# Top-32 attention with a squared-ReLU feed-forward: order of the last step and the tail, place of the negation, of a cast and of the threshold tests, and the step from which a DMA does an addition

## The chip, the cores and the metric

The kernel runs on one core of a Trainium2 chip. Its five engines work from queues of their own: TensorE (PE; its weight loads are shown as PEld), VectorE (DVE), ScalarE (ACT), GpSimd (POOL) and SyncE (SP, which here only issues DMAs). The metric is the device time of one execution in microseconds, as the median over runs.

## The reference

For each of 8 batches and 8 heads, 576 queries meet 576 keys of 64 dimensions. Of each row of scores only those stay that are at least as large as the row's 32nd largest; a softmax over them weighs the values. The result, 4608 tokens of 512 features, goes through a feed-forward with the square of a ReLU:

```python
scores = scale * np.matmul(q, k.transpose(0, 1, 3, 2))
kth = np.partition(scores, -top_k, axis=-1)[..., -top_k:-top_k + 1]
scores = np.where(scores >= kth, scores, -1000000000.0)
attn = np.exp(scores - np.max(scores, axis=-1, keepdims=True))
attn = attn / (np.sum(attn, axis=-1, keepdims=True) + 1e-09)
x = np.matmul(attn, v)            # then heads side by side: 4608 x 512
h = np.maximum(x @ w_in, 0.0)     # 4608 x 2048
out = h * h @ w_out               # 4608 x 512
```

## The kernel before

The work is cut into 144 steps (`U`). A step handles two tiles (`x` = 0, 1) of 128 queries against 576 keys. One loop over `u` writes each engine's order by hand (`pin` keeps the program order), and several steps are in flight at once.

- **Selection, DVE.** `pairs_of` and `quads_of` (L314 to L324) fold the scores by maxima and minima, so that the first of four rounds need to read only part of a row. `topk` then does four rounds of MAX8 (L373) with MATCH_REPLACE8 between (L377); the last value of the fourth round is the row's threshold. `lesser` and `both` (POOL, L347 and L338) make the smaller elements of the pairs, which the fourth round reads as well. `copy_far` (ACT, L330) saves a part (`most`) that would be overwritten in PSUM.
- **Mask, POOL.** In step u, `drop(u-1, x)` turns the threshold into a mask: `negate` (ACT, L392) gives the negatives of the row's largest value and of its threshold (`neg`); L407 on POOL writes a byte that is large where a score lies below the threshold; and that byte, read as a bfloat16 of huge magnitude, is added to the scores `s`. In steps below `EARLY` = 11 (and in the second-last step) POOL adds it itself, one L409 for each tile. Otherwise one DMA with accumulation, issued by POOL, does it for both tiles (L411).
- **Softmax and values.** `exps(u-2)` (ACT, L415) exponentiates, `turn` transposes by DMA on SP's queue (L424), `products(u-4)` (PE, L459) multiplies by the values, `invert` and `place` (DVE L473, ACT L489) normalise. In the last two steps tiles that POOL doesn't mask go through `early_exps` (ACT, L400) and `mask` (DVE, L419), and are transposed on PE (`turn_by_tensor`, L441; `turned` copies them out, L446 and L448).
- **Preparation of the next heads.** `prep_units` transposes queries and keys on PE (L174) and copies them on ACT (L175). `main` also hands a cast of the last values, `last_values` (ACT, L221), to the list `after_far`, which the same step empties after its fourth round.
- **Feed-forward.** When a block of 128 tokens is complete, `x_unit` transposes it (L527) and `block` makes four "ups" (16 matmuls each, L574, then `rl` by ACT L579 and the square) and four "downs" (4 matmuls each, L617, into the one bank `dn_ps`; after the fourth it is copied to `wide`, L625 or L623, and stored). `piece` takes one from the lists `ups` and `downs`, in turn; `dense(u, 0)` and `dense(u, 1)` call it at the end of every step. `piece(True)` leaves the evacuation for later, in the list `behind`. Blocks of 64 remaining rows of two batches go through `rem_unit`.
- **Tests.** Every 18 steps (`GROUP`) three POOL instructions (L382 to L384) compare the thresholds of the rounds and write to `flags`. At the very end DVE reduces `flags` (L855); a positive value would start a general path, which doesn't run on this data.
- **Tail.** After the loop come the masks of the last tiles, their transposes, products and placing, the last ups and downs, and the last block's downs in two halves of 256 columns (`halves`, L598).

Of the kernel before, what the change touches and what calls it, by code (L numbers as in the profile page):

```python
# [23 lines left out]
def kernel(  # L24
# [9 lines left out]
    nc = tc.nc  # L34
# [10 lines left out]
    def pin(ins):  # L45
        tc.keep_in_program_order(ins)
        return ins
# [43 lines left out]
    raw, prep = {}, {}  # L91

    fetches = []
    after_far = []

    def by_head(t):
        return t.rearrange("p (a d) -> p a d", a=2)
# [61 lines left out]
    def prep_units(i):  # L159
# [10 lines left out]
        def main(which, src):  # L170
            def go():
                tp = ps_one.tile([128, 512], f32, name="gen", bufs=2)
                for c in range(4):
                    pin(nc.tensor.transpose(tp[:, c * 128:(c + 1) * 128], src[:, c], id_f[:, :]))  # L174
                pin(nc.scalar.activation((qT, kT[:, 64:576])[which], tp[:, :], AF.Copy, scale=(scale, 1.0)[which]))  # L175
                after_far.append(lambda: last_values(which))
            return go


# [38 lines left out]
        def last_values(x):  # L218
            assert i < 6 or av_left[i - 6] == 0
            half = slice(64 * x, 64 * x + 64)  # L220
            pin(nc.scalar.activation(va[half, 4 + x, :, 0:64], by_head(v_raw[half, 512:640]), AF.Copy))  # L221
# [127 lines left out]
    GROUP = 18  # L349
    EARLY = 11  # L350
    held_m = {}

    def topk(u, rounds=(0, 1, 2, 3)):
        d = st[u]
        g = u % GROUP
        if g == 0 and 0 in rounds:
            held_m["m"] = small.tile([128, GROUP, 2, 4, 8], f32, name="m", bufs=2)
        held = held_m["m"]  # L360
        m = d["m"] = [held[:, g, :, r] for r in range(4)]
        d["ends"] = held[:, g].rearrange("p x r j -> p x (r j)")[:, :, 0:32:31]
        cat = d["cat"]
        def part(r, x):
            if r == 0:
                return cat[:, x, 0:QUAR].rearrange("p (g n) -> p g n", n=18)[:, :, 0:13]
            if r == 1:
                return cat[:, x, 0:QUAR].rearrange("p (g n) -> p g n", n=6)[:, :, 1:6]
            return cat[:, x, 0:(HALF - 24, S)[r - 2]]

        for r in rounds:
            for x in range(2):
                pin(nc.vector.max(out=m[r][:, x, :], in_=part(r, x)))  # L373
            if r == 3:
                break
            for x in range(2):
                pin(nc.vector.match_replace(out=part(r, x), in_to_replace=m[r][:, x, :], in_values=part(r, x), imm_value=NEG))  # L377
        if g == GROUP - 1 and 3 in rounds:
            f0 = 2 * (u + 1 - GROUP)
            each = held[:, :, :, :, 7].rearrange("p g x r -> p (g x) r")  # L380
            at = flags[:, f0:f0 + 2 * GROUP]
            pin(nc.gpsimd.tensor_tensor(at[:, :, 0:3], each[:, :, 3:4].broadcast_to([128, 2 * GROUP, 3]), each[:, :, 0:3], op=ALU.subtract))  # L382
            pin(nc.gpsimd.tensor_mul(at[:, :, 3], each[:, :, 3], each[:, :, 3]))
            pin(nc.gpsimd.tensor_scalar(at[:, :, 3], at[:, :, 3], scalar1=-1.0, scalar2=TINY * TINY, op0=ALU.mult, op1=ALU.add))  # L384

    def by_vector(u, x):
        return u == U - 1 or (u == U - 2 and x == 1)
# [13 lines left out]

    def drop(u, x):
        d = st[u]
        if x == 0:
            d["neg"] = negate(u, 2)
        s, byte = d["s"], gone[u % 2]
        pin(nc.gpsimd.tensor_scalar(byte[:, x, :, 1], s[:, x, :], scalar1=d["neg"][:, x, 1:2], scalar2=-HUGE, op0=ALU.add, op1=ALU.mult))  # L407
        if by_vector(u, 1) or u < EARLY:
            pin(nc.gpsimd.tensor_tensor(s[:, x, :], s[:, x, :], byte[:, x, :, :].rearrange("p n two -> p (n two)").bitcast(bf16), op=ALU.add))  # L409
        elif x == 1:  # L410
            pin(nc.gpsimd.dma_start(out=s[:, :, :].rearrange("p x n -> p (x n)"), in_=byte[:, :, :, :].rearrange("p x n two -> p (x n two)").bitcast(bf16), accum_op=ALU.add))  # L411
# [328 lines left out]
    def ok(w):  # L740
        return 0 <= w < U
# [16 lines left out]
    for u in range(U):  # L758
        at_step[0] = u
        for x in range(2):  # L760
            if ok(u - 1) and not by_vector(u - 1, x):
                drop(u - 1, x)
        quads_of(u)
        topk(u, (0,))
        if u == U - 1:
            products(u - 4)
        if ok(u + 1):
            for i, c, a in steps[u + 1]:
                while coming <= i or (coming == i + 1 and soon):
                    prepare(u)  # L770
            scores(u + 1, (lambda: in_gap(u)) if u else None)
            both(u + 1)
        if u == 0:
            in_gap(u)
        if ok(u - 4):
            invert(u - 4)
        casts_next = bool(soon) and soon[0].__name__ == "values"
        for _ in range(0 if casts_next else 2 if u < 8 else 1):
            prepare(u)
        if ok(u - 4):  # L780
            place(u - 4)
        turn_x(u)
        moves.extend(soon_moves)
        soon_moves.clear()
        if u == U - 1:
            moves.pop(0)()()
        if ok(u - 2):
            exps(u - 2, 0)
            exps(u - 2, 1)
            turn(u - 2)  # L790
        fetch(4 if u < 12 else 3)
        topk(u, (1, 2))
        if ok(u + 1):
            pairs_of(u + 1)
            copy_far(u + 1)
            lesser(u + 1)
        topk(u, (3,))
        if casts_next:
            prepare(u)
        while after_far:  # L800
            after_far.pop(0)()
        if u == U - 2:
            early_exps(u, 1)
        if u < U - 1:
            dense(u, 0)
            dense(u, 1)
        else:
            early_exps(u, 0)
            exps(u - 1, 0)
            early_exps(u, 1)  # L810
            piece(True)
            piece(True)
        load_weights(1)
    mask(U - 2, 1)
    mask(U - 1, 0)
    mask(U - 1, 1)
    while_scores.close()
    ends["pool"] = fast.enter_context(tc.tile_pool(name="ps_end", bufs=1, space=PSUM))

    def flush():  # L820
        if behind:
            behind.pop(0)()

    assert not fresh and not moves and not soon_moves
    late.append(True)
    products(U - 4)
    piece(True)
    behind.sort(key=lambda go: go.down)
    invert(U - 4)
    for u in (U - 2, U - 1):  # L830
        for x in range(2):
            turn_by_tensor(u, x)
            turned(u, x, u == U - 2)
    products(U - 2)
    products(U - 1)
    place(U - 4)
    products(U - 3)
    invert(U - 2)
    flush()
    place(U - 2)  # L840
    invert(U - 1)
    invert(U - 3)
    flush()
    place(U - 1)
    place(U - 3)
    rest = ups.pop(0)()
    turn_x(U)
    moves.pop(0)()()
    rest()
    while behind:  # L850
        flush()
    tail.append(0)
    while ups:
        ups.pop(0)()()
# [141 lines left out]
```

## Time and profile before

| | |
|---|---|
| median of 3 runs | 917.33 us (914.49 to 920.94) |
| profiled execution | 915.97 us, its span 914.1 us |
| granted TensorE clock, mean | 0.942 of full speed |
| DVE busy | 882.7 us (97%) |
| POOL busy | 777.6 us (85%) |
| ACT busy | 760.2 us (83%) |
| PE busy | 675.0 us (74%) |
| DMA moved | 163.60 MB, mean 179 GB/s |

A row of the timeline gives the start, the duration from the first to the last of the merged instructions, the engine, the line, the operation, its output and inputs with shapes, and the count; in brackets the idle time of the engine ahead of it and what ended it. A row of the waits gives who waited for whom: the total in us, how often, and the longest. A row of the windows gives a stretch, its length, the busy time of PE, PEld, DVE, ACT and POOL with counts, the granted PE clock, the busy share of the DMA engines and their GB/s. Lines (L392) are those of the kernel before; in the changed kernel they lie up to five further down.

### The profile page before, as it was taken

What the parts mean: (1) busy time and instruction counts of PE and PEld (TensorE: products, weight loads), DVE (VectorE), ACT (ScalarE), POOL (GpSimd) and SP (SyncE); (2) the same over time, 40 slices, a digit from 0 to 9 for tenths busy, and PEclk for the clock granted to TensorE, in tenths of its full rate; (3) what the DMA queues carried; (4) which work ended last, traced back from release to release, by engine and by line L of the source; (5) the groups of instructions that cost most, each with busy time, mean ns of one, the idle gap of its engine ahead of it and who ended that gap; (6) DMA issues with size and microseconds to landing.
All of it is one profiled execution on the core that took longest, in us unless ns stands there. A gap on an engine that the chain in (4) does not pass through costs nothing.

```text
span 914.1 us, 20885 instructions
## 1 busy us (share of the span) xinstructions
PE 675.0 (74%) x6188; PEld 427.2 (47%) x6264; DVE 882.7 (97%) x3632; ACT 760.2 (83%) x1755; POOL 777.6 (85%) x804
## 2 busy tenths in 40 slices
PE   6667667776786777777786777777777778878776
PEld 3333344544454445444454444454444445545454
DVE  5999999999999999999999999999999999999993
ACT  4566699889888998888987899988998888998881
POOL 7998989888988889888888888998898888888860
PEclk9999999899989999999989999999999999999999
DMA  7698799899998999899899998989989999788851
GB/s 145 106 165 142 155 184 202 192 198 194 193 202 185 196 198 195 190 175 215 178 198 182 202 199 186 205 193 196 185 192 197 199 202 196 156 166 172 163 117 39
DMA packets 290489, 163.60 MB, mean 179 GB/s; under 512 B 258112, under 2 KB 268608, under 8 KB 290368
## 3 DMA queue, kind: packets, MB, share of 16 engines
q1 hardware_dynamic: 267408, 80.29, 47.1%
q0 software_dynamic: 21616, 81.47, 40.0%
q8 instruction: 52, 0.85, 0.4%
q14 instruction: 69, 0.57, 0.2%
q10 hardware_dynamic: 1344, 0.43, 0.2%
HBM read 37.75 MB, written 9.44 MB: 52 GB/s over the span
## 4 chain that ended last, share of the span: by engine, by line
DVE 66%; issue 11%; PE 4%; DMA 3%; ACT 2%; POOL 2%; POOLq 0%; ACTq 0%
DVE m L373 27%; DVE cat L377 18%; DVE sc_b L314 6%; DVE cat L324 5%; DVE cat L323 5%; DVE most L315 4%; DMA s<-gone_a 1%; DMA s<-gone_b 1%; PE dn_ps L617 1%; DVE rsum L473 1%; PE gen L574 1%; PE sc_b L285 1%; POOL gone_b L407 0%; POOL cat L347 0%; PE end L598 0%
## 5 line engine op out<-in xcount | busy, mean ns | idle before, releaser
L373 DVE MAX8 m<-cat 128x8 f32<-128x104 f32 (+3 forms) x1152 | 438.7, 422 | 0.2 <-POOL cat L347 0.2
L377 DVE MATCH_REPLACE8 cat<-m,cat 128x104 f32<-128x104 f32 (+2 forms) x864 | 263.1, 312 | 0.0
L338 POOL TENSOR_TENSOR cat<-s 128x576 int32<-128x576 int32 (+1 forms) x144 | 238.6, 1657 | 3.1 <-ACT s L294 3.1
L347 POOL TENSOR_TENSOR cat<-cat,most 128x576 int32<-128x576 int32 (+1 forms) x144 | 195.8, 1360 | 19.6 <-ACT most L330 7.0
L285 PE MATMUL sc_b<-qkT 64*128 64x288 f32 x512 | 109.1, 501 | 95.3 <-DVE cat L324 91.2
L285 PE MATMUL sc_a<-qkT 64*128 64x288 f32 x512 | 98.2, 456 | 96.6 <-DVE most L315 62.9
L574 PEld LDWEIGHTS <-w_in 128*128 128x128 bf16 x2304 | 146.2, 101 | 39.0 <-issue 17.1
L617 PE MATMUL dn_ps<-w_out,h 128*128 128x512 bf16 x494 | 147.2, 420 | 10.3 <-issue 5.7
L294 ACT ACTIVATE s<-sc_b 128x576 f32<-128x576 f32 x144 | 93.4, 649 | 63.9 <-PE sc_b L285 57.0
L574 PE MATMUL gen<-xT,w_in 128*128 128x128 bf16 x2000 | 138.5, 226 | 2.6 <-ACT xT L533 1.4
L407 POOL TENSOR_SCALAR gone_a<-s,neg 128x576 uint8<-128x576 f32 x143 | 106.6, 745 | 21.3 <-ACT neg L392 10.8
L407 POOL TENSOR_SCALAR gone_b<-s,neg 128x576 uint8<-128x576 f32 x142 | 105.9, 746 | 18.3 <-ACT neg L392 7.7
L285 PEld LDWEIGHTS sc_a<-qkT 64*128 64x128 f32 x512 | 41.8, 188 | 124.2 <-issue 30.7
L285 PEld LDWEIGHTS sc_b<-qkT 64*128 64x128 f32 x512 | 44.7, 201 | 110.7 <-PE av_ps L459 64.1
L294 ACT ACTIVATE s<-sc_a 128x576 f32<-128x576 f32 x144 | 91.0, 632 | 3.3 <-DVE cat L317 1.7
L585 ACT ACTIVATE h<-rl 128x512 bf16<-128x512 f32 x136 | 85.7, 630 | 4.3
L579 ACT ACTIVATE rl<-gen 128x512 f32<-128x512 f32 x141 | 84.0, 596 | 2.4 <-PE gen L574 1.9
L617 PEld LDWEIGHTS <-h 128*128 128x128 bf16 x560 | 54.3, 106 | 66.2 <-issue 32.5
L459 PEld LDWEIGHTS <-wT 128*128 128x128 bf16 (+1 forms) x1600 | 54.9, 100 | 53.6 <-issue 43.9
L411 POOL DMA_DIRECT2D s<-gone_b x66 | 58.4, 884 | 21.7 <-DVE m L373 7.6
L415 ACT ACTIVATE w_two_a<-s,neg 128x576 bf16<-128x576 f32 x96 | 69.4, 781 | 6.7 <-DMA s<-gone_b 4.5
L415 ACT ACTIVATE w_two_c<-s,neg 128x576 bf16<-128x576 f32 x94 | 68.0, 781 | 8.1 <-DMA s<-gone_b 4.7
(170 smaller groups left out, 1203.1 us busy)
## 6 DMA issues: line engine op xcount, KB each, us to landing
s<-gone_b POOLq DMA_DIRECT2D x66, 576.0 KB, 4.6
s<-gone_a POOLq DMA_DIRECT2D x65, 576.0 KB, 4.7
v_raw<-in_v_dram SPq DMA_DIRECT2D x64, 128.0 KB, 3.1
k_raw<-in_k_dram SPq DMA_DIRECT2D x63, 128.0 KB, 3.3
q_raw<-in_q_dram SPq DMA_DIRECT2D x63, 128.0 KB, 3.2
out_dram<-wide SPq DMA_DIRECT2D x31, 256.0 KB, 3.1
v_raw<-in_v_dram SPq DMA_DIRECT2D x64, 32.0 KB, 3.1
w_in<-in_moe_w_in_dram POOLq DMA_DIRECT2D x8, 256.0 KB, 4.8
```

Source lines behind the costliest of these rows:

```text
L285: pin(nc.tensor.matmul(out=ps[j][:, x, 0:HALF], lhsT=lhsT, rhs=rhs, start=True, stop=True))
L294: pin(nc.scalar.activation(s[:, :, j * HALF:(j + 1) * HALF], ps[j][:, :, 0:HALF], AF.Copy))
L338: pin(tt(less, s[:, :, 0:wide].bitcast(i32), s[:, :, HALF:HALF + wide].bitcast(i32), op=ALU.add))
L347: pin(tt(less, less, d["most"][:, 0:n_h, :, :].bitcast(i32).rearrange("p h x n -> p x h n"), op=ALU.subtract))
L373: pin(nc.vector.max(out=m[r][:, x, :], in_=part(r, x)))
L377: pin(nc.vector.match_replace(out=part(r, x), in_to_replace=m[r][:, x, :], in_values=part(r, x), imm_value=NEG))
L407: pin(nc.gpsimd.tensor_scalar(byte[:, x, :, 1], s[:, x, :], scalar1=d["neg"][:, x, 1:2], scalar2=-HUGE, op0=ALU.add, op1=ALU.mult))
L415: pin(nc.scalar.activation(w_two[u % 3][:, x, 0:S], d["s"][:, x, :], AF.Exp, bias=d["neg"][:, x, 0:1]))
L574: pin(nc.tensor.matmul(out=hp[:, n * n_rows:(n + 1) * n_rows], lhsT=w_in[:, kh, (f0 + n) * 128:(f0 + n + 1) * 128], rhs=xt(kh), start=(kh ...
L579: pin(nc.scalar.activation(rl[:, :], hp, AF.Relu))
L585: pin(nc.scalar.activation(h2, flat, AF.Square))
L617: pin(nc.tensor.matmul(out=op[:, :], lhsT=held["h2"][:, f, c * 128:(c + 1) * 128], rhs=w_out[:, f, :], start=(f == 0), stop=(f == NF - 1)))
```

## The change

- The casts of `last_values` go through a second list, `next_far`, and run one step later.
- The three test instructions become five of 128 x 36 elements (`tests`); one runs per step on POOL, after `lesser`; what is left runs after the loop.
- `negate` moves from the start of the next step's `drop` to between `dense(u, 0)` and `dense(u, 1)`.
- The DMA adds the mask from step 9 on (`EARLY - 2`) instead of 11; nothing else that depends on `EARLY` changes.
- In the last step two `piece()` calls stand behind `products(u - 4)`. In the changed order of instructions these are the last two downs of the block of remainder rows, whose copy to `wide` falls to ACT; the two `piece(True)` calls later in the step are then both ups of the second-last block.
- In the tail the `piece(True)` behind `products(U - 4)` is gone, inversions follow their products, one postponed evacuation runs ahead of `place(U - 4)` and one after the transposes of the last block.

```diff
@@ prep_units: main
-                after_far.append(lambda: last_values(which))
+                next_far.append(lambda: last_values(which))
@@ topk
-            pin(nc.gpsimd.tensor_tensor(at[:, :, 0:3], each[:, :, 3:4].broadcast_to([128, 2 * GROUP, 3]), each[:, :, 0:3], op=ALU.subtract))
-            pin(nc.gpsimd.tensor_mul(at[:, :, 3], each[:, :, 3], each[:, :, 3]))
-            pin(nc.gpsimd.tensor_scalar(at[:, :, 3], at[:, :, 3], scalar1=-1.0, scalar2=TINY * TINY, op0=ALU.mult, op1=ALU.add))
+            for r in range(3):
+                tests.append(lambda r=r: nc.gpsimd.tensor_tensor(at[:, :, r], each[:, :, 3], each[:, :, r], op=ALU.subtract))
+            tests.append(lambda: nc.gpsimd.tensor_mul(at[:, :, 3], each[:, :, 3], each[:, :, 3]))
+            tests.append(lambda: nc.gpsimd.tensor_scalar(at[:, :, 3], at[:, :, 3], scalar1=-1.0, scalar2=TINY * TINY, op0=ALU.mult, op1=ALU.add))
@@ drop
-        if x == 0:
+        if "neg" not in d:
             d["neg"] = negate(u, 2)
...
-        if by_vector(u, 1) or u < EARLY:
+        if by_vector(u, 1) or u < EARLY - 2:
@@ the loop over u
         if u == U - 1:
             products(u - 4)
+            piece()
+            piece()
...
             lesser(u + 1)
+            if tests:
+                pin(tests.pop(0)())
         topk(u, (3,))
         if casts_next:
             prepare(u)
         while after_far:
             after_far.pop(0)()
+        after_far.extend(next_far)
+        next_far.clear()
...
             dense(u, 0)
+            st[u]["neg"] = negate(u, 2)
             dense(u, 1)
@@ after the loop
+    while tests:
+        pin(tests.pop(0)())
     mask(U - 2, 1)
...
     products(U - 4)
-    piece(True)
-    behind.sort(key=lambda go: go.down)
-    invert(U - 4)
     for u in (U - 2, U - 1):
         for x in range(2):
             turn_by_tensor(u, x)
             turned(u, x, u == U - 2)
+    invert(U - 4)
     products(U - 2)
+    invert(U - 2)
     products(U - 1)
+    invert(U - 1)
+    behind.pop(0)()
     place(U - 4)
     products(U - 3)
-    invert(U - 2)
-    flush()
     place(U - 2)
-    invert(U - 1)
     invert(U - 3)
-    flush()
     place(U - 1)
     place(U - 3)
-    rest = ups.pop(0)()
+    behind.append(ups.pop(0)())
     turn_x(U)
     moves.pop(0)()()
-    rest()
+    behind.pop(0)()
+    behind.append(ups.pop(0)())
     while behind:
-        flush()
+        behind.pop(0)()
```

More of the change, by code (lines that the diff above doesn't have):

```diff
@@ L93 @@
     fetches = []
-    after_far = []
+    after_far, next_far = [], []
     def by_head(t):
@@ L351 @@
     held_m = {}
+    tests = []
     def topk(u, rounds=(0, 1, 2, 3)):
@@ L818 @@
     ends["pool"] = fast.enter_context(tc.tile_pool(name="ps_end", bufs=1, space=PSUM))
[L820 to L824, printed above, removed]
+    assert not fresh and not moves and not soon_moves and len(behind) == 2 and len(ups) == 2
     late.append(True)
     products(U - 4)
-    piece(True)
-    behind.sort(key=lambda go: go.down)
-    invert(U - 4)
     for u in (U - 2, U - 1):
```

## The prediction

> **What bounds the kernel now.** I read the page first, then stages by windows, the waits of VectorE (DVE), and the instructions in order of time where DVE has gaps.
>
> ```profile
> PE 675.0 (74%) x6188; PEld 427.2 (47%) x6264; DVE 882.7 (97%) x3632; ACT 760.2 (83%) x1755; POOL 777.6 (85%) x804
> ...
> core 0: us, PE busy (x) PEld busy (x) DVE busy (x) ACT busy (x) POOL busy (x), PEclk, DMA share, GB/s
> 0.00:40.00 40.00, 26.24 (x121) 13.43 (x124) 30.81 (x126) 18.64 (x42) 33.31 (x73) 1.00 0.71 130
> 40.00:80.00 40.00, 27.77 (x189) 13.26 (x191) 39.48 (x160) 24.35 (x61) 36.41 (x41) 0.96 0.97 162
> 80.00:120.00 40.00, 27.90 (x242) 16.30 (x244) 37.53 (x153) 29.57 (x71) 36.55 (x35) 0.96 0.73 146
> ...
> 300.00:400.00 100.00, 73.66 (x697) 47.63 (x702) 100.00 (x421) 88.29 (x204) 88.21 (x88) 0.94 0.93 191
> ...
> 880.00:914.00 34.00, 22.98 (x249) 16.66 (x250) 17.50 (x45) 13.07 (x31) 5.44 (x6) 0.89 0.24 51
> ```
>
> DVE is the wall: from 120 to 880 us it hardly pauses (100.00 of 100.00 us in the stretch shown), and the change takes no instruction from it there. So only DVE's 31.4 us of idle time (914.1 - 882.7) can be won: 9.2 us before 40, 0.5 + 2.5 us from 40 to 120, 16.5 us after 880, and what is left of the sum, 2.7 us, in the 760 us between. The head before 40 us waits for first loads and transposes, which the change leaves alone. I cost the rest in three parts: tail, steps 8 to 12, steady steps.
>
> **Tail.** Rows of PE, DVE and ACT in order of time, each engine by itself:
>
> ```profile
> 876.06 1.89 PE L617 MATMUL dn_ps<-w_out,h 128*128 128x512 bf16 x7
> 877.78 0.47 PE L459 MATMUL av_ps<-vau_b,wT 128*128 128x65 bf16 x10
> 881.61 0.43 PE L527 MATMUL gen<-id_h,x_tok 128*128 128x128 bf16 x2 [3.24 <-ACT x_tok L489]
> 887.24 0.67 PE L441 MATMUL end<-id_h,w_two_b 128*128 128x128 bf16 x9
> 891.37 0.55 PE L527 MATMUL end<-id_h,x_tok 128*128 128x128 bf16 x4 [0.51 <-ACT x_tok L489]
> 895.32 1.06 PE L574 MATMUL end<-xT,w_in 128*128 128x128 bf16 x16
> 896.43 0.81 PE L617 MATMUL dn_ps<-w_out,h 128*128 128x512 bf16 x3
> 899.86 5.17 PE L617 MATMUL dn_ps<-w_out,h 128*128 128x512 bf16 x16 [2.62 <-DVE wide L623]
> 904.96 0.19 PE L863 MATMUL gen<-ones,worst 128*1 128x1 f32 x2
> ...
> 885.50 1.76 DVE L419 SCALAR_TENSOR_TENSOR w_two_c<-s,m,e 128x576 bf16<-128x576 f32 x2
> 897.66 1.34 DVE L855 TENSOR_REDUCE worst<-flags 128x1 f32<-128x1152 f32 x1
> 899.11 0.69 DVE L623 COPY wide<-dn_ps 128x512 f32<-128x512 f32 x1
> ...
> 881.24 0.52 ACT L489 ACTIVATE x_tok<-av_ps,rsum 128x64 bf16<-128x64 f32 x2 [0.68 <-DVE rsum L473]
> 889.13 0.62 ACT L579 ACTIVATE rl<-gen 128x512 f32<-128x512 f32 x1
> 889.61 0.55 ACT L489 ACTIVATE x_tok<-end,rsum 128x64 bf16<-128x64 f32 x2
> ...
> 896.30:899.80 3.50, 0.89 (x5) 0.31 (x4) 3.26 (x5) 0.60 (x1) 0.00 (x0) 0.98 0.02 5
> 899.80:905.00 5.20, 5.14 (x18) 1.86 (x17) 0.01 (x1) 0.00 (x0) 0.00 (x0) 0.69 0.23 50
> ```
>
> Today the third-last block of the feed-forward (the remainder rows) leaves its last four L617 matmuls (896.43; the profile lost one) for after the last L574 group. The next block's sixteen need the same single dn_ps bank, and its copy L623 stands on DVE behind the reduction L855, so PE waits 2.62 us. In the changed order of instructions all eight remaining L617 matmuls stand in the last step ahead of the x_tok transposes, their copy on ACT. Three gains follow.
>
> *Queue.* The sixteen then follow the L574 groups: they start where the four start now, 899.86 - 896.43 = 3.43 us earlier. What was moved is covered: eight L617 take 877.78 - 876.06 = 1.72 us at full clock, and PE is idle 3.24 us ahead of 881.61; the copy (0.69 us on DVE, about as much on ACT) falls into ACT's 0.68 us wait ahead of 881.24. Without that cover the x_tok chain would lose at most that 0.7.
>
> *Clock.* The sixteen took 904.96 - 899.86 = 5.10 us at a granted clock of 0.69; at the rate of the eight they take 2 x 1.72 = 3.44. With no wait in front of them I expect the full rate: 1.66 us. If the clock is low for another reason: 0.
>
> The Trainium skill ("TensorE: Matmul & The Clock Gate", "What's actually happening") says that the clock falls after an idle window of about 3.4 us, free-running. A wait of 2.62 us doesn't fill one, so read strictly the slow sixteen would have another cause and stay slow, and the whole sum below would be 7.3 instead of 9.0. The trace, 0.98 in the stretch up to the end of the wait and 0.69 behind it, speaks for the wait.
>
> *Front.* Two L574 groups of the second-last block run in the last step, one after the other, instead of one, four L617 and another; the transposes L441 of w_two_b, today at 887.24, can start up to 0.9 us earlier. Those of the last half of w_two_c still wait for the last mask (885.50 + 1.76 = 887.26). Only one of the two postponed rl evacuations stands ahead of the last x_tok on ACT instead of two (889.61 - 889.13 = 0.48 us). I bound the gain at 891.37 by 0 (mask alone) and 0.48 + 0.62 = 1.1 (a whole evacuation as well) and take 0.8, nearer the upper end since both chains shorten.
>
> Tail: 3.43 + 1.66 + 0.8 = 5.9, bounds 3.4 and 6.2. The number of L574 groups behind the last x_tok stays at five, and what follows the last L598 stays.
>
> **Steps 8 to 12.** Waits of DVE from 40 to 120 us, and the rows on ACT, POOL and DVE behind them:
>
> ```profile
> DVE sc_b L314 <- ACT s L294: 0.5, 1, 0.5
> ...
> DVE cat L323 <- ACT most L330: 2.3, 3, 1.4
> DVE m L373 <- POOL cat L347: 0.2, 1, 0.2
> ...
> 77.51 0.32 ACT L221 ACTIVATE vau_e<-v_raw 64x128 bf16<-64x128 f32 x1 [4.83 <-DMA v_raw<-in_v_dram]
> 98.65 1.44 ACT L415 ACTIVATE w_two_c<-s,neg 128x576 bf16<-128x576 f32 x2 [1.61 <-DMA s<-gone_b]
> 106.16 1.44 ACT L415 ACTIVATE w_two_a<-s,neg 128x576 bf16<-128x576 f32 x2 [1.45 <-DMA s<-gone_a]
> ...
> 86.10 1.28 POOL L409 TENSOR_TENSOR s<-s,gone_a 128x576 f32<-128x576 f32 x1
> 94.40 0.95 POOL L411 DMA_DIRECT2D s<-gone_b  x1 [0.31 <-DVE cat L323]
> 100.26 0.90 POOL L411 DMA_DIRECT2D s<-gone_a  x1 [0.31 <-POOL gone_a L407]
> ```
>
> Two causes. ACT stood 4.83 us at L221 for values not yet loaded; the scores' copies behind it came late, and DVE lost 0.5 at L314 and part of the 2.3 at L323. `next_far` puts this cast a step later (6 us), past the landing at 77.5. Then POOL comes late into the first steps whose `s` is summed by DMA: two L409 a step (2.56 us) against one L411 of 0.9. The DMA sent at 94.40 and 100.26 lands after ACT wants it, `most` comes late, DVE waits. The switch at step 9 instead of 11 spares POOL 2 x (2.56 - 0.95 - 0.3) = 2.6 us, so those DMAs leave some 2.6 us earlier than today, more than the 1.61 and 1.45 that ACT waited. All of 0.5 + 2.3 + 0.2 = 3.0 can go; at the least the part of the cast, about 0.9 (0.5, and half of the 0.9 that the longest L323 wait, 1.4, leaves of 2.3). The two new accumulating DMAs must land before ACT's L415 two steps later; the existing ones took 98.65 - 94.40 = 4.3 and 106.16 - 100.26 = 5.9 us, less than a step. I take 2.6.
>
> **Steady steps.** Negation and tests:
>
> ```profile
> 649.85 0.58 ACT L579 ACTIVATE rl<-gen 128x512 f32<-128x512 f32 x1
> 650.46 0.63 ACT L585 ACTIVATE h<-rl 128x512 bf16<-128x512 f32 x1
> 650.99 0.19 ACT L392 ACTIVATE neg<-m 128x4 f32<-128x4 f32 x1
> 651.28 1.56 POOL L407 TENSOR_SCALAR gone_a<-s,neg 128x576 uint8<-128x576 f32 x2 [1.24 <-ACT neg L392]
> 649.38 0.43 DVE L323 TENSOR_TENSOR cat<-sc_b,most 128x288 f32<-128x288 f32 x1
> ...
> L382 POOL TENSOR_TENSOR flags<-m 128x108 f32<-128x108 f32 x8 | 4.3, 536 | 1.7 <-DVE m L373 1.7
> L383 POOL TENSOR_TENSOR flags<-m 128x36 f32<-128x36 f32 x8 | 2.6, 319 | 0.0
> ```
>
> The maxima that L392 needs are ready when L323 starts (649.38). Today L392 waits behind both dense evacuations; between them it goes at 649.85, and L407 on POOL, and the DMA behind it, leave 650.99 - 649.85 = 1.14 us earlier. Where ACT comes early, L392 now waits for DVE with the second evacuation (0.58 + 0.63 = 1.2 us) queued behind it, and behind that the copies of the next scores; PE's next gen bank comes free later too. The 786 us from 94.40, in step 12, to 880 hold 131 steps, 6.0 us each; ACT has 11.7 us in 100 to spare, 0.70 a step, so a wait below that is hidden.
>
> The tests: today 1.17 us at once per 18 steps (536 + 319 ns, and as much as L383 once more for L384); as five of about 0.32 they cost 1.6 in five steps. 8 x 0.43 = 3.4 us more on POOL in all, inside its 11.8 us of slack per 100; if POOL were the path, those 3.4 would show. The last five run behind the last maxima, beside the tail, whose reduction comes only at 897.66. DVE's 2.7 us of gaps here come from late DMAs and slow PE stretches; an earlier POOL closes a few. I take a gain of 0.5, bounds 2.7 gained and 3.4 lost.
>
> **Sum.** 5.9 + 2.6 + 0.5 = 9.0 us. The profiled execution took 915.97 us (span 914.1 and 1.9 around it): 906.97. It lay 1.36 below the median of the runs shown, 917.33, so for the median 908.3. Bounds: 6.2 + 3.0 + 2.7 = 11.9 gained, 905.4; 3.4 + 0.9 - 3.4 = 0.9 gained, 916.4.
>
> **Rivals.**
> - *Half the tail.* The queue is gained, but clock and front are not (the strict reading of the clock rule would do that), or the new DMAs of steps 9 and 10 come late, since the DMA share from 40 to 80 us is 0.97: 3.4 + 2.6 + 0.5 = 6.5 gives 910.8; 3.4 + 0.9 + 0 = 4.3 gives 913. For it: 16 matmuls at 0.69. Against: 0.98 up to the end of the wait.
> - *Everything closes.* POOL's earlier start removes nearly all steady gaps as well: 905.4. Against: one of the gaps sits at a slow stretch of PE, which the change doesn't touch.
> - *The negation holds ACT* (slower). In place of L407 waiting for L392, ACT waits in L392, and the second evacuation, the scores' copies and `most` follow late, so DVE waits at L323. It decides from a wait of 0.70 us a step; it can at most cost 1.2 - 0.7 = 0.5 us a step, and in a third of the 131 steps behind step 12 that is 22 us: 908.3 + 22 = 930. Against: a second evacuation of 1.2 us begun with L323 is over while DVE still has three of the step's four rounds to do before L314 reads the next scores.
> - *Nothing on the path moves*: not likely, as the order of instructions shows the moved pieces.
>
> **How the numbers follow.** Forecast 0.48 (906.5 to 910), half the tail 0.25 (910 to 915), everything closes 0.19 (below 906.5), negation holds ACT 0.08. 908.3 is 1.0% below 917.33; 1% is about what a measurement of this kernel can tell from no change, and it would be 908.2. So just under half of the forecast, 0.23, and one more case, 0.19, in all with a little for run scatter 0.45, are faster by over 1%; slower 0.07; within 1% the rest, 0.48. The range runs from 904.0 (all closes, and the runs' lower scatter) to 915.0.
>
> **What would show it.** PE without a wait between the last L574 and the sixteen L617, at clock 1.00, in 3.5 us; eight L617 ahead of the x_tok transposes of the last step; the L441 and L527 transposes up to 1 us closer to the last mask. No wait of ACT at L221, none at L415 near steps 11 and 12, DVE's waits from 40 to 120 us below 0.5 us. Waits of L407 on L392 mostly gone, and more waits of L392 on DVE, with DVE still at 100 of 100 us. Wrong it would be if DVE has new waits at L314 or L323 in the steady steps, or if PE still idles before the sixteen.

## The result, and the profile after

The changed kernel takes 906.97 us (median of 6 runs, 906.43 to 908.46), the kernel before 919.71 us in the same session (median of 6, 914.49 to 920.94). The ratio is 0.9874, with a 95% interval of 0.9849 to 0.9898: 1.3% faster. The forecast was 908.3 us. The profiled execution of the changed kernel took 907.14 us; its span is 905.0 us against 914.1, so 9.1 us are gone where the sum had 9.0.

Windows of the changed kernel (columns as before: length, then busy time and instructions of each engine, granted clock, DMA share, GB/s):

```profile
40.00:120.00 80.00, 58.03 (x445) 31.10 (x450) 79.30 (x327) 56.95 (x136) 72.73 (x76) 0.96 0.98 176
300.00:400.00 100.00, 73.55 (x705) 47.95 (x710) 100.00 (x412) 87.89 (x204) 88.06 (x88) 0.93 0.91 191
120.00:880.00 760.00, 563.34 (x5398) 363.91 (x5463) 758.84 (x3158) 673.49 (x1557) 668.03 (x665) 0.95 0.91 190
...
0.00:879.93 879.93, 647.62 (x5961) 408.36 (x6037) 869.23 (x3609) 749.20 (x1732) 774.38 (x813) 0.95 0.91 186
```

Of the kernel before; the last window of both ends at the first mask of the last step (DVE L419 before, L421 after):

```profile
120.00:880.00 760.00, 570.15 (x5396) 367.52 (x5458) 757.36 (x3153) 674.59 (x1555) 665.92 (x652) 0.94 0.92 190
...
0.00:884.79 884.79, 654.55 (x5958) 412.53 (x6034) 869.97 (x3610) 750.90 (x1733) 775.28 (x801) 0.94 0.90 184
```

The first mask comes at 879.93 instead of 884.79, and from there to the end of the span it takes 25.07 us instead of 29.31. So the loop gave 4.86 us and the tail 4.24; the sum had 3.1 and 5.9. In the loop DVE's idle time went from 14.82 to 10.70 us. From 40 to 120 us it fell from 2.99 to 0.70, and from 120 to 880 us from 2.64 to 1.16; the first 40 us gave 0.36 (31.17 us busy instead of 30.81). The other 0.74 of the 4.86 us is busy time: up to the first mask DVE's own instructions took 869.23 us in all instead of 869.97.

The tail of the changed kernel, PE, DVE and ACT in order of time, each by itself, and two windows:

```profile
875.70 1.04 PE L619 MATMUL dn_ps<-w_out,h 128*128 128x512 bf16 x4 [1.06 <-ACT h L587]
878.80 3.57 PE L576 MATMUL gen<-xT,w_in 128*128 128x128 bf16 x32 [0.68 <-ACT xT L535]
...
882.73 1.15 PE L443 MATMUL end<-id_h,w_two_b 128*128 128x128 bf16 x9
...
887.17 0.49 PE L529 MATMUL end<-id_h,x_tok 128*128 128x128 bf16 x4
891.38 1.06 PE L576 MATMUL gen<-xT,w_in 128*128 128x128 bf16 x16
892.49 3.40 PE L619 MATMUL dn_ps<-w_out,h 128*128 128x512 bf16 x15
895.82 0.19 PE L868 MATMUL gen<-ones,worst 128*1 128x1 f32 x2
...
879.93 0.83 DVE L421 SCALAR_TENSOR_TENSOR w_two_b<-s,m,e 128x576 bf16<-128x576 f32 x1
881.01 0.82 DVE L421 SCALAR_TENSOR_TENSOR w_two_c<-s,m,e 128x576 bf16<-128x576 f32 x1 [0.24 <-ACT e L402]
882.34 0.82 DVE L421 SCALAR_TENSOR_TENSOR w_two_c<-s,m,e 128x576 bf16<-128x576 f32 x1 [0.51 <-ACT e L402]
...
876.77 0.60 ACT L627 ACTIVATE wide<-dn_ps 128x512 f32<-128x512 f32 x1 [1.03 <-PE dn_ps L619]
877.27 0.51 ACT L491 ACTIVATE x_tok<-av_ps,rsum 128x64 bf16<-128x64 f32 x2
...
892.40:895.90 3.50, 3.45 (x18) 1.44 (x16) 2.61 (x4) 0.60 (x1) 0.00 (x0) 1.00 0.00 0
877.80:884.40 6.60, 5.92 (x60) 5.73 (x60) 4.65 (x11) 5.13 (x9) 2.49 (x6) 0.50 0.43 88
```

Three things are to be seen. The last sixteen L619 (the record of the first is missing) follow the last L576 group at once, at clock 1.00. In the last step there is a new chain: the last four of the eight moved L619 wait 1.06 us for `h`, ACT's copy `wide` waits 1.03 us for them, and `x_tok` stands behind that copy. The early exponentials L402 stand behind `x_tok`, and the masks now wait 0.24 and 0.51 us for them. And from 877.7 to 884.5 us PE runs at half rate, clock 0.50; before it did so from 882.6 to 886.0, half as long.

The waits of the changed kernel (us in total, times, longest):

```profile
ACT neg L394 <- DVE m L374: 72.8, 96, 3.1
...
POOL gone_a L409 <- ACT neg L394: 4.8, 8, 1.4
...
POOL gone_b L409 <- ACT neg L394: 0.6, 2, 0.3
...
DVE cat L323 <- ACT most L330: 0.5, 2, 0.3
```

And of the kernel before:

```profile
ACT neg L392 <- DVE m L373: 19.6, 15, 2.6
...
POOL gone_a L407 <- ACT neg L392: 10.8, 20, 1.2
...
POOL gone_b L407 <- ACT neg L392: 7.7, 16, 1.2
...
DVE cat L323 <- ACT most L330: 3.8, 7, 1.4
```

POOL's waits on the negation went from 18.5 to 5.4 us; ACT's waits in the negation grew from 15 to 96. DVE, from 300 to 400 us, stays at 100.00 of 100.00.

### The profile page after: what moved, and what is told of

The parts are those of the page before. It is cut to its first block, busy times and chain, and to the rows that moved or that the text cites. A ratio compares the mean times of both kernels' runs of the same rounds, so it can differ in the third digit from the quotient of the medians.

```text
span 905.0 us, 20910 instructions
## 1 busy us (share of the span) xinstructions
PE 666.7 (74%) x6188; PEld 424.3 (47%) x6264; DVE 881.3 (97%) x3631; ACT 759.6 (84%) x1756; POOL 776.7 (86%) x818
## 4 chain that ended last, share of the span: by engine, by line
DVE 73%; issue 12%; ACT 6%; PE 5%; DMA 3%; POOL 2%; SPq 0%; POOLq 0%; ACTq 0%; DVEq 0%
DVE m L374 30%; DVE cat L378 19%; DVE sc_b L314 7%; DVE most L315 5%; DVE cat L324 5%; DVE cat L323 5%; ACT s L294 1%; DVE rsum L475 1%; PE dn_ps L619 1%; DMA s<-gone_b 1%; DMA k_raw<-in_k_dram 1%; DMA s<-gone_a 1%; PE sc_b L285 1%; ACT rl L581 1%; PE gen L576 1%
## 5 line engine op out<-in xcount | busy, mean ns | idle before, releaser
L374 DVE MAX8 m<-cat 128x8 f32<-128x104 f32 (+3 forms) x1152 | 450.5, 443 | 0.0
L378 DVE MATCH_REPLACE8 cat<-m,cat 128x104 f32<-128x104 f32 (+2 forms) x864 | 271.6, 332 | 0.0
L285 PE MATMUL sc_b<-qkT 64*128 64x288 f32 x512 | 105.7, 487 | 93.3 <-DVE cat L324 89.1
L576 PEld LDWEIGHTS <-w_in 128*128 128x128 bf16 x2304 | 148.0, 102 | 38.7 <-issue 15.9
L619 PE MATMUL dn_ps<-w_out,h 128*128 128x512 bf16 x494 | 143.2, 410 | 8.9 <-issue 5.8
L576 PE MATMUL gen<-xT,w_in 128*128 128x128 bf16 x2016 | 139.9, 226 | 2.8 <-ACT xT L535 1.8
L394 ACT ACTIVATE neg<-m 128x4 f32<-128x4 f32 (+1 forms) x145 | 29.9, 206 | 74.0 <-DVE m L374 72.8
L378 DVE MATCH_VALUE_LOAD cat<-m,cat 128x8 f32 x864 | 83.7, 97 | 0.0
L619 PEld LDWEIGHTS <-h 128*128 128x128 bf16 x560 | 52.9, 104 | 61.9 <-issue 25.3
```

What stands on the lines that cost most here:

```text
L285: pin(nc.tensor.matmul(out=ps[j][:, x, 0:HALF], lhsT=lhsT, rhs=rhs, start=True, stop=True))
L576: pin(nc.tensor.matmul(out=hp[:, n * n_rows:(n + 1) * n_rows], lhsT=w_in[:, kh, (f0 + n) * 128:(f0 + n + 1) * 128], rhs=xt(kh), start=(kh ...
L619: pin(nc.tensor.matmul(out=op[:, :], lhsT=held["h2"][:, f, c * 128:(c + 1) * 128], rhs=w_out[:, f, :], start=(f == 0), stop=(f == NF - 1)))
```

## The experiments

Each kernel is either the changed one with something undone or put elsewhere, or the one before with something added. Ratios are to the kernel before on the same chip. Diffs against the changed kernel unless said otherwise.

### Loop alone, tail alone

The loop of the changed kernel with the old tail and without the two new `piece()` calls:

```diff
         if u == U - 1:
             products(u - 4)
-            piece()
-            piece()
...
+    piece(True)
+    behind.sort(key=lambda go: go.down)
...  (the rest of the tail as before)
```

> The changed kernel with the last step's pieces and the tail as before; all edits of the loop stay. Theory: the two parts add up, the loop brings DVE to the first L419 mask 4.9 us earlier (884.79 before, 879.93 in the changed kernel) and the tail is the old one: span 914.1 - 4.9 = 909.2 us, with PE waiting 2.6 us for the copy again. Rival: the early arrival is worth something only with the new tail, since the old one waits for ACT and PE anyway: span above 911 us.

911.22 us (median of 9, 910.31 to 912.62), ratio 0.9932 (0.9909 to 0.9955). PE of this kernel at the sixteen, and a window of the last step:

```profile
895.01 5.30 PE L619 MATMUL dn_ps<-w_out,h 128*128 128x512 bf16 x16 [2.61 <-DVE wide L625]
...
875.70:882.30 6.60, 5.92 (x48) 4.62 (x48) 5.42 (x15) 4.12 (x7) 3.81 (x6) 0.50 0.38 46
```

With the old tail the wait of 2.61 us is back, and the sixteen take 900.24 - 895.01 = 5.23 us again. The last step has a stretch at clock 0.50 of 6.8 us, as long as in the changed kernel. Its first mask came at 878.69, 6.1 us earlier than before and not 4.9, and from there the rest took 30.81 us, 1.5 longer than before with the same tail; the span of 909.5 us, close to the 909.2 expected, is the sum of the two deviations.

The other half, against the kernel before: the old loop with the new pieces in the last step and the new tail.

```diff
             products(u - 4)
+            piece()
+            piece()
...  (and the tail of the changed kernel)
```

> The kernel before with the new pieces in the last step and the new tail alone. Theory: the mask starts near 884.8 us as before, the rest is 4.2 us shorter (25.1 instead of 29.3 us): span 909.9 us. Inside it the queue gains 3.4, the clock 1.8 and the front loses about 0.9. Rival (the prediction's own terms): the front gains 0.8 and the loop's edits spoiled it in the changed kernel, so the rest is 23.4 us and the span 908.2 us.

913.16 us (median of 10, 908.70 to 917.08), ratio 0.9934 (0.9901 to 0.9966). From the first mask at 885.02 to the end it took 25.2 us, as in the changed kernel (25.07). The two halves multiply to 0.9932 x 0.9934 = 0.9867, the whole is 0.9874: loop and tail add up, each worth about half. PE and DVE of this kernel in the last step, and a window:

```profile
881.77 1.04 PE L617 MATMUL dn_ps<-w_out,h 128*128 128x512 bf16 x4 [1.55 <-ACT h L585]
...
884.82 1.95 PE L574 MATMUL gen<-xT,w_in 128*128 128x128 bf16 x32 [0.69 <-ACT xT L533]
887.72 0.68 PE L441 MATMUL end<-id_h,w_two_b 128*128 128x128 bf16 x9 [0.65 <-ACT w_two_b L415]
...
887.03 0.82 DVE L419 SCALAR_TENSOR_TENSOR w_two_c<-s,m,e 128x576 bf16<-128x576 f32 x1 [1.22 <-ACT e L400]
...
884.80:889.50 4.70, 3.42 (x60) 3.12 (x60) 2.97 (x5) 4.67 (x9) 1.46 (x3) 1.00 0.57 117
```

Here the same 32 ups ran at full clock (1.95 us instead of 3.57), and PE then waited for the late weights from ACT. From the first mask to the x_tok transposes (892.09) it took 7.07 us, 6.58 before: in this kernel the moved pieces delay the masks through ACT, without any loss of clock. The masks wait 1.22 and 0.51 us for `e` here, and not 0.24 and 0.51; ACT was later by more than the copy, likely because it had waited 0.91 us for a DMA of the mask one step earlier (877.93).

### The moved copy put later

If the chain `h` - four downs - `wide` - `x_tok` is the loss, it goes away when the second down piece is issued behind the x_tok transposes of the last step and its copy behind the early exponentials:

```diff
         if u == U - 1:
             products(u - 4)
             piece()
-            piece()
...
         if u == U - 1:
-            moves.pop(0)()()
+            copy_x = moves.pop(0)()
+            last_wide = downs.pop(0)()
+            copy_x()
...
             early_exps(u, 1)
+            last_wide()
             piece(True)
```

> The changed kernel with the second of the two moved pieces issued behind the x_tok transposes of the last step, and its copy on ACT behind the early exponentials. Theory: the front lost because the last four L617 wait for h on ACT and their copy stands ahead of x_tok on ACT; then x_tok comes 0.9 us earlier, the two ups too, the masks no longer wait for e (0.8 us), and the span falls by 0.8 to 1.3 us, to 903.7 to 904.2 us. Rival: the low clock of PE in the two ups is what lost the front; it stays low after PE's wait ahead of the ups, the span stays within 0.4 us of 905.0 us.

905.63 us (median of 4, 904.16 to 906.24), ratio 0.9855 (0.9804 to 0.9906). ACT, PE and DVE of this kernel, and a window:

```profile
877.13 0.52 ACT L491 ACTIVATE x_tok<-av_ps,rsum 128x64 bf16<-128x64 f32 x2 [0.68 <-DVE rsum L475]
...
878.63 3.55 PE L576 MATMUL gen<-xT,w_in 128*128 128x128 bf16 x32
886.10 0.50 PE L529 MATMUL end<-id_h,x_tok 128*128 128x128 bf16 x4
...
880.70 0.79 DVE L421 SCALAR_TENSOR_TENSOR w_two_b<-s,m,e 128x576 bf16<-128x576 f32 x1
881.41 1.64 DVE L421 SCALAR_TENSOR_TENSOR w_two_c<-s,m,e 128x576 bf16<-128x576 f32 x2
...
878.70:882.00 3.30, 3.30 (x34) 3.30 (x33) 3.30 (x7) 3.27 (x6) 1.15 (x2) 0.50 0.29 57
```

`x_tok` waits for DVE's reciprocal only, the masks run without a pause, and from the first mask to the last x_tok transposes it takes 886.10 - 880.70 = 5.40 us instead of 7.24. The span is 903.9 us, 1.1 below that of the changed kernel: the mask itself comes 0.77 later than there, the rest is 1.9 shorter. The median is 1.3 us below the changed kernel's; the intervals of the two ratios overlap, so this is shown by the rows and the spans more than by the times.

The span is as expected, but not all of that gain is the copy's. The ups still run at half rate (3.55 us), but here the clock is back at 1.00 from 882.1 us on, after a stretch of 3.4 us; in the changed kernel the stretch is 6.8 us long, PE has no pause from 878.80 to 885.2, and its L443 run at half rate too (1.15 us for nine). The traces of the kernels below that undo or change one edit of the loop, and have the last step and tail of the changed kernel, take copy and clock apart. A window of the kernel before, and three rows of the kernel with the switch undone:

```profile
882.60:886.00 3.40, 3.27 (x20) 2.25 (x20) 3.40 (x9) 3.37 (x7) 1.72 (x3) 0.50 0.25 51
...
884.30 0.68 PE L443 MATMUL end<-id_h,w_two_b 128*128 128x128 bf16 x9 [0.64 <-ACT w_two_b L417]
...
888.72 0.50 PE L529 MATMUL end<-id_h,x_tok 128*128 128x128 bf16 x4
...
882.59 0.82 DVE L421 SCALAR_TENSOR_TENSOR w_two_b<-s,m,e 128x576 bf16<-128x576 f32 x1
```

| kernel (us) | half rate in the last step | masks wait for `e` | first mask to x_tok transposes | first mask to the end |
|---|---|---|---|---|
| before | 3.4 | 0 | 6.58 | 29.31 |
| loop alone (old tail) | 6.8 | 0 | 7.83 | 30.81 |
| changed; three spread | 6.8 | 0.75; 0.69 | 7.24; 7.21 | 25.07; 25.14 |
| cast undone, three at once, five at once | 3.4 | 0.68 to 0.71 | 6.08 to 6.16 | 23.81 to 24.05 |
| switch undone, negation undone | none | 0.66 to 0.68 | 6.12 to 6.13 | 23.91 to 24.08 |
| late copy; late copy with old negation | 3.4 | 0 | 5.40; 5.48 | 23.20; 23.66 |

With an equal stretch of half rate, the copy ahead of `x_tok` costs 0.6 to 0.8 us in front of the x_tok transposes, about what the masks wait for `e`. A stretch of 6.8 instead of 3.4 us costs 1.1 more, and 1.25 in the old tail. None or one of 3.4 makes no difference: at full clock PE waits for ACT instead (0.64 us above).

### PE kept busy in the old wait

The kernel before, with twelve matmuls of constants, whose result nobody reads, in the place where PE waited 2.62 us:

```diff
+        if len(downs) == 8:
+            hp = ps_one.tile([128, 512], f32, name="gen", bufs=2)
+            for n in range(12):
+                pin(nc.tensor.matmul(out=hp[:, :], lhsT=id_h[:, :], rhs=fill[:, :], start=(n == 0), stop=(n == 11)))
```

> The kernel before with twelve matmuls of 128 x 512 on constants (their result is read by nobody) on PE between the remainder block's last four L617 and the next sixteen, in the wait for the copy. Theory: the sixteen run at half rate because PE idled; filled, they take 3.4 instead of 5.1 us, granted clock about 1.0, span 914.1 - 1.7 = 912.4 us. Rival (a wait of 2.6 us is too short to lower the clock, something else does): they still take about 5.1 us and the span stays at 914.1 us.

917.59 us (median of 10, 912.53 to 921.12), ratio 0.9999 (0.9969 to 1.003). PE of this kernel, and two windows:

```profile
903.44 2.75 PE L864 MATMUL gen<-fill,id_h 128*128 128x512 bf16 x12
906.22 3.61 PE L617 MATMUL dn_ps<-w_out,h 128*128 128x512 bf16 x16
909.76 0.19 PE L867 MATMUL gen<-ones,worst 128*1 128x1 f32 x2
...
665.00:670.00 5.00, 2.79 (x27) 1.76 (x25) 4.61 (x18) 1.66 (x6) 4.53 (x5) 1.00 1.27 113
906.20:909.80 3.60, 3.58 (x18) 1.50 (x17) 0.00 (x0) 0.00 (x0) 0.00 (x0) 1.00 0.33 73
```

With the wait filled the sixteen run at clock 1.00 and take 909.76 - 906.22 = 3.54 us instead of 5.10. So the wait of 2.6 us was what lowered the clock. From the first mask to the end this trace takes 28.24 us instead of 29.31. The time of the whole kernel doesn't show these 1.6 us, since its runs lie 8.6 us apart; in the profiled one DVE lost 5.79 us in a single stall (below).

### Cast and switch undone

```diff
-                next_far.append(lambda: last_values(which))
+                after_far.append(lambda: last_values(which))
```

> The changed kernel with the last_values cast in its own step again. Theory: ACT waits 4 to 6 us at L221 near 75 us for v_raw, DVE waits at L314 and L323 behind it; DVE's waits from 40 to 120 us rise by 0.3 to 1.9 us (what the traces of before and of two kernels with its loop show there) and the time by as much over 906.97. Rival: with POOL's earlier start the wait of ACT is absorbed: no change.

908.28 us (median of 9, 907.44 to 910.93), ratio 0.989 (0.986 to 0.9921). ACT and the waits from 40 to 120 us of this kernel:

```profile
77.69 0.32 ACT L221 ACTIVATE vau_e<-v_raw 64x128 bf16<-64x128 f32 x1 [5.02 <-DMA v_raw<-in_v_dram]
...
DVE cat L323 <- ACT most L330: 1.1, 2, 0.8
```

```diff
-        if by_vector(u, 1) or u < EARLY - 2:
+        if by_vector(u, 1) or u < EARLY:
```

> The changed kernel with the DMA adding the mask from step 11 on as before. Theory: two more L409-type additions a step make POOL late, the first DMAs leave 2.6 us or more later, ACT waits for them at the exponentials near 98 and 106 us, DVE loses about 2 us; time 906.97 + 2 = 909. Rival: the earlier negation alone lets POOL catch up, and DVE loses less than 0.5 us.

909.17 us (median of 9, 907.19 to 911.26), ratio 0.9914 (0.9887 to 0.994). ACT and DVE of this kernel:

```profile
97.63 1.44 ACT L417 ACTIVATE w_two_c<-s,neg 128x576 bf16<-128x576 f32 x2 [1.25 <-DMA s<-gone_b]
105.20 1.44 ACT L417 ACTIVATE w_two_a<-s,neg 128x576 bf16<-128x576 f32 x2 [2.54 <-DMA s<-gone_a]
...
106.97 0.46 DVE L323 TENSOR_TENSOR cat<-sc_b,most 128x288 f32<-128x288 f32 x1 [1.47 <-ACT most L330]
```

Each brings back its own waits of before: the cast 5.02 us on ACT and 1.1 on DVE at L323 (median +1.3 against the changed kernel), the switch 1.25 and 2.54 on ACT and, at the last of them, 1.47 on DVE (median +2.2). By the times alone neither is beyond the intervals; the rows are what decides.

### Negation undone

```diff
             dense(u, 0)
-            st[u]["neg"] = negate(u, 2)
             dense(u, 1)
```

> The changed kernel with the negation behind both dense pieces again (at the start of the next step's drop). Theory: the mask DMAs leave up to 1.1 us later in heavy steps, ACT now and then waits for one at the exponentials, DVE behind it: DVE's waits from 120 to 870 us rise from about 0.5 to 2 us or more, and the runs scatter again over several us (914 to 924 for the kernel before, 906.4 to 908.5 for the changed one), with a median 1 to 4 us above 906.97. Rival: the scatter came from the start (cast and switch): the runs stay within 2 us and the median within 0.5 us.

905.58 us (median of 4, 904.86 to 907.97), ratio 0.9865 (0.9812 to 0.9918). Waits of this kernel:

```profile
POOL gone_a L409 <- ACT neg L394: 9.3, 17, 1.4
...
POOL gone_b L409 <- ACT neg L394: 4.6, 8, 1.1
```

The theory that the earlier negation was worth something falls: POOL's waits are back (13.9 us), and the time is not longer. The same edit on the kernel with the late copy gave no difference either:

> The changed kernel with the second moved piece and its copy late, as in the run with the late copy, and the negation behind both dense pieces as before. Theory: the negation's place is worth nothing, since a DMA that leaves up to 1.1 us later still lands in time once the tests are spread out: 905 us, as with the late copy alone (905.63), within 1 us. Rival: the early negation is worth 1 us or more: 906.7 us or above.

905.78 us (median of 5, 904.92 to 906.84), ratio 0.9854 (0.9824 to 0.9885), against 905.63 with the new place. It is also a second measurement of the late copy: 0.9855 and 0.9854.

### The tests, in four forms

Back to three at once:

```diff
-            for r in range(3):
-                tests.append(...)   # and two more
+            pin(nc.gpsimd.tensor_tensor(at[:, :, 0:3], ...))   # and two more, as before
```

> The changed kernel with the three threshold tests at once again. Theory: 1.2 us at once on POOL every 18 steps is absorbed by its slack: time within 0.5 us of 906.97, no scatter. Rival: the burst is what makes single mask DMAs late: DVE waits at L323 after some of the eight groups, median up by over 1 us, scatter of several us.

909.50 us (median of 9, 904.70 to 913.98), ratio 0.99 (0.9865 to 0.9935). The five tests alone, one a step, in the kernel before:

> The kernel before with the five tests, one a step, as its only change. Theory (from the run with the three tests put back, which scattered over 9 us as the kernel before does): three tests at once hold POOL for 1.2 us, the mask DMA behind them leaves late, in some runs lands after ACT wants it, and DVE stands; spread out they take this away: runs within 4 us, median 2 to 3 us below the kernel before in the same job. Rival: the scatter needs cast, switch or negation as well: median within 1 us of before, scatter of 8 us or more.

920.45 us (median of 12, 915.35 to 922.33), ratio 1.0017 (0.9996 to 1.0038): nothing, and the expected gain did not come. Five tests at once, a step later:

```diff
             lesser(u + 1)
-            if tests:
+            while tests:
                 pin(tests.pop(0)())
```

> The changed kernel with all five tests at once, in the step after the group, in the place where it runs one. Theory (the burst on POOL does the harm): 1.6 us at once, the median as with three at once, 909 to 910, scatter of 8 us or more. Rival (the harm is that the three stand behind maxima of their own step, between lesser and drop): median within 1 us of 906.97, scatter below 4 us.

908.84 us (median of 6, 907.92 to 916.59), ratio 0.9904 (0.9866 to 0.9941). Three tests, one a step:

```diff
-            for r in range(3):
-                tests.append(lambda r=r: nc.gpsimd.tensor_tensor(at[:, :, r], ...))
+            tests.append(lambda: nc.gpsimd.tensor_tensor(at[:, :, 0:3], ...))
```

> The changed kernel with three tests instead of five (the first on 108 elements a row, 0.54 us), still one a step. Theory: what counts is one a step, not the cut into five: within 0.6 us of 906.97, scatter below 4 us. Rival: also 0.54 us at once makes a mask DMA late: median up by 1 us or more.

909.86 us (median of 6, 904.96 to 914.22), ratio 0.9892 (0.9852 to 0.9932). What differs among these kernels is the spread. The kernels with the new loop and five tests one a step (the changed one, loop alone, late copy, cast, switch and negation undone, late copy with old negation; 46 runs) stay each within 1.9 to 4.1 us. The others spread wider: tail alone over 8.4 us, filler 8.6, three at once 9.3, five at once 8.7, three spread 9.3, the tests alone in the old loop 7.0, the kernel before 6.5 in its six runs and 8.0 to 10.1 in the 17 to 24 runs beside the experiments. These spreads rest on few runs: five at once has five runs within 1.2 us and one at 916.59. The lowest time of three at once (904.70) is even below that of the changed kernel (906.43), so the old tests need not cost anything; some executions meet a stall that others don't.

What the stall is, shows where a profiled execution has one. ACT and DVE of the kernel with three spread tests, and a window:

```profile
90.67 1.44 ACT L416 ACTIVATE w_two_a<-s,neg 128x576 bf16<-128x576 f32 x2 [7.22 <-DMA s<-gone_b]
...
92.44 0.46 DVE L323 TENSOR_TENSOR cat<-sc_b,most 128x288 f32<-128x288 f32 x1 [6.25 <-ACT most L330]
...
84.00:88.00 4.00, 1.21 (x4) 0.68 (x4) 2.18 (x5) 0.00 (x0) 2.47 (x3) 1.00 1.24 78
```

One DMA that adds the mask lands late, 12.1 us after its issue at 78.57; ACT waits 7.22 us for it, `most` behind it is late, and DVE stands 6.25 us. This is the first of the two DMAs that the switch to step 9 adds. The second of them was late for ACT by 1.10 us in the changed kernel's own profile (at 91.19), without a wait of DVE. In the filler kernel the same chain stands at 675.40 us: 6.68 us on ACT, 5.79 on DVE. There the DMA of the mask needed 11.3 us from issue to landing, a transpose in the same stretch 11.6 and a load of `k_raw` 9.7, with a DMA share of 1.27 at 113 GB/s (window above) where the loop as a whole moves 190. So the transfers of such a stretch are late together. The stalls do not lie just anywhere. Five traces have a wait of DVE at L323 of over 1.5 us behind 120 us: in tail alone (3.15 us at 668.92), filler (5.79) and tests alone (1.61 at 667.46) it is the 109th of the 144, in three at once the 111th (2.43 at 676.65), and only in five at once is it far away (1.84 at 793.87). Why such a stretch comes in some executions, and why five tests one a step in the new loop kept it away in 46 runs, the runs do not settle: the pieces of it by themselves (tests alone, spread alone, five at once) don't do it.

## Why the prediction was right, and where not

*The sum* was right (9.0 expected, 9.1 in the spans), but by two errors against each other, and that they cancelled is luck: the loop gave 1.8 more, the tail 1.7 less. Neither is firm to a microsecond. The same loop reached its first mask at 878.69 (loop alone) and 880.70 (late copy), so 6.1 and 4.1 us before the old one; and five traces with the same tail took 23.81 to 24.08 us for it, 5.2 to 5.5 less than before, where 5.9 was expected.

*Queue: right.* The sixteen follow the last L576 group; from the start of that group to them it takes 892.49 - 891.38 = 1.11 us instead of 899.86 - 895.32 = 4.54. That is 3.43, the number of the sum. (Both it and the sum read a start about 0.2 late, since a first record is missing each time. With all on record, as with the cast undone, it takes 892.45 - 891.56 = 0.89 us, so the queue gave 3.65.)

*Clock: right.* The sixteen took 895.82 - 892.49 = 3.33 us at clock 1.00 instead of 5.10: 1.77 gained, 1.66 expected (3.55 us and 1.55 with all sixteen on record). The filler run shows the cause by itself. The strict reading of the rule in the Trainium skill ("TensorE: Matmul & The Clock Gate", "What's actually happening"), an idle window of about 3.4 us, does not hold in this case: 2.6 us were enough, in all three traces that have the wait (before, loop alone, tests alone).

*Front: wrong, in sign in the profiled execution.* I expected +0.8; it was -0.9: first mask to x_tok transposes 6.58 us before, 7.24 after, and from there to the last L576 group 3.95 and 4.21. Two steps failed. The first is "what was moved is covered". I had counted the durations of the moved downs and of the copy against idle time ahead of `x_tok`, and had not asked what the downs wait for. The last four need `h` of the last up of their block, which ACT delivers only then; the copy can't start until they are done, and ACT, which runs its instructions in the written order, has `x_tok` and the exponentials behind it. This costs 0.6 to 0.8 us, as the late copy shows, about the 0.7 that I had named as the price without cover. The second is the clock of the last step, for which the sum had no term. Its half-rate stretch was 6.8 us long in the changed kernel's profile instead of 3.4 before, and that cost 1.1. With the same tail and a stretch of 3.4 us or none the x_tok transposes come 6.08 to 6.16 us behind the first mask, 0.4 to 0.5 sooner than before, and the front is +0.2 in all. What decides the length of the stretch stays open. The tail of the profiled execution is thus 3.43 + 1.77 - 0.9 = 4.3, 4.24 by the windows.

*Steps 8 to 12: right.* DVE's idle time from 40 to 120 us fell by 2.3 (2.6 expected); the waits at L221 and at L415 near steps 11 and 12 are gone (one of 1.10 us is new, for the DMA of step 10), and each of the two undone edits brings its own back.

*Steady steps: the size low, the reason not shown.* DVE's idle time from 120 to 880 us fell by 1.5, not 0.5. One trace of each kernel doesn't settle this size: from 120 to 870 us DVE stood 0.45, 1.16 and 2.53 us in the three with the changed loop (loop alone, changed, late copy), and 2.64, 4.02 and 8.17 in the three with the old one (before, tail alone, filler). The reason given, an earlier POOL through the earlier negation, is not what did it: with the negation back, in two kernels, nothing is lost. Its cost is nil too: 96 waits of ACT, and DVE does not feel them, so the rival in which the negation holds ACT did not come. The row that shrank is DVE's wait at L323: 3.8 us in all before, of which 2.3 lay between 40 and 120 and 1.5 behind, and 0.5 in all after. Behind 120 that is 1.0 us less of waiting for late `most`; what made these come less late in the steady steps stays open, and the spread of the runs belongs to the same question. The rest of what the loop gave beyond the sum, 0.36 us in the first 40 and 0.74 in DVE's busy time, stood in no term of the prediction.

*Tests:* alone they change nothing, as argued. That the spread of the runs may hang on their form, together with the new loop, was not foreseen.

*From the profiled run to the median.* I put the profiled execution of before 1.36 us below its median and added that to the forecast. With six runs it lay 3.74 below (915.97 and 919.71; the medians beside the experiments, of 17 to 24 runs, were 916.78, 919.16 and 919.42), while the changed kernel's lay 0.17 above its own. So of the 12.7 us between the medians 8.8 lie between the two profiled executions (915.97 and 907.14); the other 3.9 belong to the spread, most runs of before being longer than the profiled one. That they are stalls like those above is likely, since the three other traces with the old loop (tail alone, filler, tests alone) have one of 1.6 to 5.8 us, but no trace of such a run of the kernel before was taken. Lowest against lowest the kernels differ by 914.49 - 906.43 = 8.1.

*Half the tail* was near the truth for the tail of the profiled execution (4.24, where it had 3.4 and the forecast 5.9), but for another reason than it gave, and the loop made it up. Its other condition, that the new DMAs of steps 9 and 10 come late, did occur, in one trace: the stall of 6.25 us with three spread tests.

## What to carry to other kernels

When work is moved into a gap, its duration fitting is not enough: look what it waits for, and what stands behind it on every engine it touches; a copy on an in-order engine that waits for a matmul that waits for an evacuation delays all that is queued there, here by 0.6 to 0.8 us. A wait of PE ahead of a burst of matmuls can cost twice, its own length and the slower clock behind it, so closing it can be worth more than the wait. Before a cause is read from one trace, look at the same stretch in every trace that has it unchanged: here that took apart the copy and the clock. And where runs of a kernel spread wide, subtract from the profiled execution's own time and ask separately whether the change alters the spread.

## What the runs showed of the hardware

A pause of PE of 2.6 us was followed by a lower clock on the next sixteen matmuls in all three traces that have it (5.10, 5.23 and 5.23 us), and in none of the eleven where PE works up to them (3.54 to 3.55 us where all sixteen are on record).

In windows of 0.1 us over the 40 us that end 6 us before the end of each of the fourteen traces, the clock is at 0.50 in fifteen stretches: twelve of 3.4 us and three of 6.8. The length of the pauses ahead doesn't tell which: after pauses of 1.41, 0.78 and 0.69 us in the last step (1.40, 0.78 and 0.68 in the last case) there was no such stretch with the switch undone, one of 3.4 us with three or five tests at once, and one of 6.8 with three spread. What decides it is open.

And transfers of one stretch can all be late together, the mask's DMA by up to 12.1 us from issue to landing, while the DMA queues show a share above 1.2 at 78 to 113 GB/s instead of 190.
